# A gate's matmul folded into another projection as one more column, and a new hand-ordered list of steps, in a one-core kernel that mixes a state-space model with linear attention

## The chip, the core and the metric

The kernel runs on one core of a Trainium2 chip. The metric is the device time of one execution in microseconds (us); of several runs the median is taken. Each core has five engines with programs of their own: TensorE (PE in the profile; PEld is its loading of weights, which overlaps the matmuls), VectorE (DVE), ScalarE (ACT), GpSimd (POOL) and SyncE (SP, which here only starts DMAs). They meet through semaphores. Matmul results go to PSUM, eight banks of 128 x 512 f32; everything else lives in SBUF.

## The reference

x is 1 x 2048 x 512 in bf16 (2048 tokens). What is computed, cut to what matters:

```
g  = sigmoid(x @ gate_w)                              # one number per token
# a: diagonal complex state-space model, 512 states
Bu = x @ B_bar.T ;  h[t] = Lam_bar * h[t-1] + Bu[t]   # over the 2048 tokens
a  = 2 * Re(h @ C.T) + x * Dskip
# b: linear attention, 32 heads of 16, not causal
q, k, v = split(x @ wqkv)
phi(u)  = concat(softmax(u @ w_phi), softmax(-u @ w_phi))     # 32 features a head
kv = sum_t phi(k)[t] v[t].T ;  z = sum_t phi(k)[t]
o  = (phi(q) @ kv) / (phi(q) . z + eps)
b  = o @ wo
out = g * a + (1 - g) * b
```

## The kernel before, in words

**Tiles.** The tokens are cut into 16 tiles of 128; a tile holds one half of the tokens of one residue mod 8. On the side of q and of the output the tiles come in the order of the list `order`, so that n is a place and `ti = order[n]` the tile; k and v go through them as 0 to 15. Features are made for groups of tiles: k's in groups of 2, 2, 4, 4 and 4, q's in four groups of 4 (G0 to G3).

**Steps.** Every piece of work is a generator `st_*` or `feat_*`, and each `yield` ends a step. The string `ORDER` is the program: a token such as `k0` runs the next step of that generator, `@3` gives it PSUM bank 3 (`@51` the banks 5 and 1), and `:D` says that a copy or a scaling of this step goes to DVE and not to ACT. The last lines of the kernel walk through it:

```
for tok in ORDER.split():
    ...
    sel["eng"] = "dve" if eng == "D" else "act"
    sel["banks"] = [int(b) for b in banks]
    next(st[tok])
```

A manual schedule is on for all five engines: each of them executes its instructions in the order in which the list issues them, and waits where a buffer or a bank isn't ready. No planner moves anything. DMA queues work the same way: SP's loads, transposing loads and stores, and POOL's adding DMAs, go in list order.

**The names.** What the list's tokens do, in rough order of time:

- *Head.* `Lk` loads two of the four row blocks of k's weight on SP, while ACT's own queue has loaded the other two ahead of the list (`wk_nat`). `Z` is a matmul on zeros, used by no one (L316). `W00` and `W01` transpose the blocks that come by SP, `W10` and `W11` those that come by ACT's queue (L299), each with a copy out of PSUM; `T0`, `T1` transpose the first two tiles of x, the others come by transposing DMAs (`Lx`) into `xT`. `B` builds the block-diagonal matrix `BD` of w_phi. `f0` to `f3` multiply it into k's weight (L443), giving `Wk2`: 480 columns, 32 heads of 15, since a softmax needs only differences to the first feature. `w0` to `w3` do the same for q's weight, giving `Wq2`.
- *Projections.* `k`, `v`, `q` of a tile are each four matmuls of 128 x 128 weights (a block of `xT`) against 480 or 512 columns (`tile_mm`, L483), then a copy out of PSUM (`evac`, L129) into `Xq` or `vx`.
- *Features.* `x`, `n`, `e`, `s` for k and `X`, `N`, `E`, `S` for q: maximum and minimum over the features of a head as trees on DVE and the subtractions (L542, L548), exponentials on ACT (L554, two instructions of 2048 columns for four tiles), sums as a tree on DVE (L531), logarithm and exponential of the sums on ACT, and the multiplication on DVE (L569, L581). Four tiles of q then go through two transposing DMAs on SP into `phT`.
- *Keys and values.* `a` accumulates kv and z in two PSUM banks over all 16 tiles (L599). Between them stand the gate's matmuls (L603): four per tile with one column, into sixteen spare columns of the second bank. `Y` masks the sums into `KVm`.
- *Gate.* One generator `G` takes the sixteen columns from PSUM: a clamp on DVE, an exponential on ACT, an addition and a reciprocal on DVE (L743 on). It leaves `nge` (the clamped logit with its sign turned) and `G`, both 128 x 16, one column a tile.
- *State-space model.* `b` and `g` multiply x into the states and step through the eight residues on PE (L613, L625), `z` scans over the 256 chunks on DVE, `H`, `h`, `p` expand the result to all residues with scalings on ACT or DVE and, for j of 0 and 1, adding DMAs on POOL; `c` scales C, with an adding DMA (L648).
- *Output, per tile.* `y`: sixteen matmuls with C (L816) into a bank `py`; for tiles that aren't in `XD` four more against `Dd`, a diagonal matrix of Dskip (L823), so that x * Dskip is added in PSUM. `o`: eight matmuls of phi(q) with `KVm` (L835); on ACT the logarithm of the denominators (`ld`, L839) and an exponential with the bias `nge` (`rd`, L842), which makes exp(-logit) / denominator; on DVE the product `on` (L848). `O` transposes `on` by a DMA on SP into `oT` for two tiles (for one, at tiles 14 and 15). `t`: four matmuls with Wo (L875) accumulate on the same bank `py`; then `ot` = py * G on ACT (L881) or DVE (L883). That is the gate: G * (a + exp(-logit) * b) = g * a + (1 - g) * b. `R` stores two tiles.
- *Skip term of tiles in `XD`.* Before, `XD = (8, ..., 14)`: `u` makes `xd` = x * G * Dskip on DVE (L854), from token rows loaded by `Ld` into `WKV`, where the weights of k and v were; `t` then adds it with `scalar_tensor_tensor` on DVE (L879). Of tile 15, the last, PSUM and output are cut at column 384 (`LASTCUT`), so that the parts may go to two engines and two store queues.

Around the change, then, the order of the work is set by the list alone, and everything but the list is a few lines: those of the gate in `st_a` and `st_G`, and those that read `G` and `nge`.

Of the kernel before, what the change touches and what calls it, by code (L numbers as in the profile page):

```python
# [20 lines left out]
P = 128  # L21
# [8 lines left out]
b001@1 s0 x2 s0 s0 Lc b000 b101@3 x2 w3@4 k9 s0 n2 k13@2 x2 k10 b011 Lo n2 x2 n2 g001@7 M2 b010 b001 Lc e2 s1 x3 s1 n3  # L30
k14@5 x3 g000@1 v6 w1@0 s1 g001 x3 g000 n3 k13 s1 n3 g010@2 c1:D c1:D Lc Lc e2 g001 g010 s0 g000 s1 g011@6 g011 x0z:D
x3 n3 k14 c2 b101 D s1 s2 c2:D s2 g011 g010 g010 D g011 s2 a0@51 a0 c0 v2@7 w3 g011 g011 k12@3 c0:D w0@4 v2 g010 k12
g010 w2@6 w2 s2 g100@7 g100 x3 s2 n3 c3 c3:D x4 w1 Ld z0 z0 b110@6 x4 z0 n4 z0 w0 z0 n4 b111@2 g101@4 g101 s1 b110 z0
e3 g101 n4 q2@6 z0 n4 z0 q1@0 c3:D x4 z0 x4 e3 s3 z0 s3 g100 b111 c0 a1 a1 g111@4 s2 x4 n4 q3@3 g111 g111 g111 g110@2
H0:D g110 g110 q2 H0 c2 Ld Ld g110 s3 q0@6 b211@7 H0 s3 q1 s2 H0 g110 c0 q0 b201@0 q3 g110 c1 X0 N0 g111 g111 v7@6 H0
z1 z1 X0 s3 b200@2 g201@4 b201 N0 c2 v7 z1 X0 z1 z1 z1 s3 N0 b211 z1 b200 z1 g200@0 b210@6 g201 q4@7 e4 b210 X0 v4@2
N0 e4 z1 z1 H1 s2 g200 g200 g201 H1 g210@6 g211@3 g210 s4 H1 c1 g211 g210 q7@4 v4 s4 h0 h0 H1 H1 g210 h0 a2 a2 a2 a2
h1 h1 s4 s3 q4 s3 s4 g211 g211 q5@2 q5 q6@0 g211 X0 N0 q7 q6 g211 g210 X1 b300@7 g210 z2 b300 z2 p00:D z2 z2 z2 b311@4
p00 z2 b301@0 E0 X1 z2 b301 z2 E0 X1 v13@7 g301@6 s4 q9@0 b310@3 z2 b311 s4 z2 g301 g300@2 H2 S0 X1 S0 g301 g300 H2:D
S0 h1 b310 g310@4 g300 N1 S0 p10 c3 S0 h1:D h1 N1 s4 g311@6 q9 g311 g311 g311 g310 g310 g310 S0 S0 s4 p10 p10 H2 q10@2  # L40
g311 S0 g311 g310 g310 z3 z3 v13 H2 p00 H2 z3 z3 z3 v8@0 v8 v10@3 h0 z3 v10 p10 N1 v12@4 v12 z3 z3 S0 S0 h0 q8@0 p10
q8 z3 z3 v9@7 v9 v14@3 h2 h2:D H3:D H3:D p00:D v14 v15@0 v15 h2 v11@4 H3 a3 N1 a3 v11 a3 a3 a4 H3 q11@4 H3 a4 a4 h2 h2
a4 X1 N1 Y Y p11 h3 p11 y1@0 G y1 h3 y1 h3 Y Y q11 q10 X2 N2 G h3 h3 END q12@2 o1@4 o0@6 E1 X2 E1 o0 q14@1 q14 N2 o1
y6@3 y6 X2 N2 X2 S1 o0 o0 S1 q12 o1 y6 S0 p01 o1 q15@1 S1 N2 q15 q13@2 q13 p11 o3@6 y0@1 o3 S1 S1 p00 y0 X2 p30 o2@4
S1 o2 S1 o2 y0 N2 S1 o2 N3 o3 G Ld Ld E2 E2 y7@2 y7 S1 y7 y3@4 y3 y3 N3 p20 p01 X3 G o3 S2 O0 t0 t0 t1 t1 y5@5 S1 S1
X3 o4@6 O1 S2 o4 o4 N3 R0 o5@0 S2 S2 o5 o5 o4 o5 O2 S2 S2 N3 X3 X3 p30 y5 y5 y4@6 y4 S2 S2 o6@0 p01 p11 p01 o6 o6 X3
y2@7 p20 N3 E3 E3 p20 o6 p20 p20 t3 y2 y2 t2 t5 y4 t2 t3:D t4 t4 S2 S2 y10@4 o9@0 o9 o8@6 p30 p30:D p30 p11 y10 u9 S3
t5 o8 o8 o9 o8 o9 y11@5 o7@6 p01 y11 y9@0 S2 p21 S3 o7 S3 S3 O4 o7 o7 p31 p21:D y9 S3 S3 y8@1 S3 o10@6 R1 u8 o10 o10
S3 S3 y8 o10 p31 t8 o11@6 O3 t9 S3 S3 t6 o11 o11 p21 p31 t8 t9 y12@1 t7 p31:D y14@0 t6 t7 o11 o12@6 o12 p21 O5 p21
o13@2 u11 p31 y14 o12 o12 o13 y12 o13 R2 o14@6 o13 O6 o14 o14 o14 R4 u10 O7 y13@2 y13 o15@6 o15 o15 o15 t10 t10 R3 t11  # L50
t13 t11 u12 O8 u13 t12 t12 t13 u14 R5 t14 t14 R6 y15@54 y15 y15 t15 t15:D t15 R7 t15 R8 R8
# [4 lines left out]
XD = (8, 9, 10, 11, 12, 13, 14)  # L56
# [14 lines left out]
def kernel(  # L71
# [88 lines left out]
    Wq2 = const.tile([P, KT, DF], BF16, name="Wq2")  # L160
# [3 lines left out]
    gw_b = const.tile([P, KT], BF16, name="gw_b")  # L164
# [275 lines left out]
    def fold(W2, WT, dtile):  # L440
        pf = bank([P, DF], F32, "pf")
        for j in range(KT):
            MM(out=pf[:, j * DF // KT:(j + 1) * DF // KT], lhsT=WT[:, j, dtile * P:(dtile + 1) * P], rhs=BD[:, j].rearrange("p g f -> p (g f)"), start=True, stop=True)  # L443
# [37 lines left out]
    def tile_mm(pt, ti, W, k0=0, k1=KT):  # L481
        for kt in range(k0, k1):
            MM(out=pt[:], lhsT=xT[:, kt, ti * P:(ti + 1) * P], rhs=W[:, kt, :], start=(kt == 0), stop=(kt == KT - 1))  # L483
# [107 lines left out]
    def st_a(n):  # L591
        first, L = KGROUPS[n]
        for u in range(L):
            n_ = first + u
            ti = KO[n_]
# [6 lines left out]
            for kt in range(KT):  # L602
                MM(out=live["acc"][1][:, 4 * KVW + ti:4 * KVW + ti + 1], lhsT=xT[:, kt, ti * P:(ti + 1) * P],  # L603
                   rhs=gw_b[:, kt:kt + 1], start=False, stop=(n_ == NTI - 1 and kt == KT - 1), skip_group_check=True)
# [138 lines left out]
    def st_G():  # L743
        VS(out=nge[:], in0=live["acc"][1][:, 4 * KVW:4 * KVW + NTI], scalar1=-Z_MAX, scalar2=-1.0, op0=ALU.max, op1=ALU.mult)
        yield
        aexp(out=G[:], in_=nge[:], func=ACT.Exp)
        yield
        VS(out=G[:], in0=G[:], scalar1=1.0, scalar2=None, op0=ALU.add)
# [78 lines left out]
    def st_o(n):  # L827
        ti = order[n]
        op_ = pools["op"][1]
# [7 lines left out]
        yield  # L837
        ld = op_.tile([P, 2, 16], F32, name="ld")
# [3 lines left out]
        aexp(out=rd[:], in_=ld[:], func=ACT.Exp, scale=-1.0, bias=nge[:, ti:ti + 1])  # L842
# [8 lines left out]
    def st_u(n):  # L851
        ti = order[n]
        live["xd", n] = pools["op"][1].tile([P, D], F32, name="xd", bufs=2)
        nc.vector.scalar_tensor_tensor(out=live["xd", n][:], in0=xl(n), scalar=G[:, ti:ti + 1], in1=Drow[:], op0=ALU.mult, op1=ALU.mult)  # L854
# [11 lines left out]
    def st_t(n):  # L866
        ti = order[n]
# [5 lines left out]
        for py, (c, w) in zip(pys, [(0, D)] if len(pys) == 1 else LASTCUT):  # L873
# [4 lines left out]
            if n in XD:  # L878
                nc.vector.scalar_tensor_tensor(out=ot, in0=py[:], scalar=G[:, ti:ti + 1], in1=live["xd", n][:, c:c + w], op0=ALU.mult, op1=ALU.add)  # L879
            elif sel["eng"] == "act":  # L880
                nc.scalar.mul(out=ot, in_=py[:], mul=G[:, ti:ti + 1])  # L881
# [73 lines left out]
```

## Time and profile before

| | before |
|---|---|
| device time, median of 3 runs | 151.08 us (150.99 to 151.36) |
| span of the profiled execution | 149.4 us |
| PE busy | 142.8 us (96%), 1010 instructions |
| PE weight loads | 73.8 us (49%) |
| DVE busy | 139.0 us (93%), 338 instructions |
| ACT busy | 125.1 us (84%), 222 instructions |
| POOL busy | 26.6 us (18%), 42 instructions |
| DMA | 20.14 MB, mean 135 GB/s |

The profile records one execution, from its first instruction to its last (its span). The runs' median is 1.7 us longer than this span: a run's time also holds what lies around the span. A line of groups gives busy time, engine, source line, operation, output and inputs with their shapes, a count, and in brackets the idle time ahead of them with what ended it. A line of single rows begins with the start in us from the span's start and the duration. Matmuls overlap in the array, so a duration is longer than the distance to the next start; where costs are added up, distances are used.

### The profile page before, as it was taken

The numbers are of one execution on the slowest core, as the hardware profiler recorded it, in microseconds if no ns is written. First come the engines' busy times: TensorE is split into PE (matmuls) and PEld (weight loads), VectorE is DVE, ScalarE is ACT, GpSimd is POOL, SyncE is SP. The second block draws the span as 40 slices with busy tenths as digits, with TensorE's granted clock in tenths as the row PEclk, the third lists the DMA queues.
The fourth block names the chain that finished last, engine by engine and source line by source line (L and its number), as shares of the span: only waits on it lengthen the run. The fifth ranks groups of instructions, "written<-read, shape, count | busy, mean of one in ns | idle before, by whom it ended". The sixth has DMA issues, their size and how long they took to land.

```text
span 149.4 us, 2839 instructions
## 1 busy us (share of the span) xinstructions
PE 142.8 (96%) x1010; PEld 73.8 (49%) x1010; DVE 139.0 (93%) x338; ACT 125.1 (84%) x222; POOL 26.6 (18%) x42
## 2 busy tenths in 40 slices
PE   6999999999999999999999999999999999999980
PEld 2844444545545444464444467555444554455450
DVE  2899999999999999999999999999999999986880
ACT  3479999999999999999999999999989996552000
POOL 7403700000000341022605236011004200000000
PEclk9999999999999999999999999999999999999999
DMA  4999999991220174008274999908999996998742
GB/s 118 222 235 174 142 202 176 246 189 33 54 91 0 26 114 77 0 0 140 38 107 70 166 175 183 210 7 133 103 238 218 184 186 77 227 207 197 209 148 71
DMA packets 52959, 20.14 MB, mean 135 GB/s; under 512 B 44496, under 2 KB 52432, under 8 KB 52944
## 3 DMA queue, kind: packets, MB, share of 16 engines
q1 hardware_dynamic: 48000, 15.44, 53.1%
q0 software_dynamic: 4000, 4.20, 18.6%
q10 hardware_dynamic: 944, 0.31, 0.8%
q8 instruction: 8, 0.13, 0.4%
q14 instruction: 7, 0.06, 0.1%
HBM read 2.91 MB, written 2.10 MB: 33 GB/s over the span
## 4 chain that ended last, share of the span: by engine, by line
ACT 67%; PE 24%; issue 3%; DVE 2%
ACT EE L554 15%; PE PS L816 11%; ACT Xq L129 9%; PE PS L875 7%; ACT CT L436 6%; ACT vx L129 5%; ACT dg L436 4%; ACT H L129 3%; ACT vv L129 3%; ACT eb L129 3%; ACT Bn L129 3%; PE PS L316 2%; PE PS L835 2%; ACT lg L562 2%; ACT m L436 1%
## 5 line engine op out<-in xcount | busy, mean ns | idle before, releaser
L554 ACT ACTIVATE EE<-EE 128x2048 bf16<-128x2048 bf16 x16 | 32.5, 2066 | 0.2 <-DVE EE L548 0.2
L483 PE MATMUL PS<-WKV,xT 128*128 128x480 bf16 (+1 forms) x128 | 29.3, 373 | 0.2 <-DMA xT<-in_A_x_dram 0.2
L483 PEld LDWEIGHTS <-xT 128*128 128x128 bf16 x192 | 18.1, 98 | 19.4 <-DMA xT<-in_A_x_dram 0.7
L129 ACT CAST Xq<-PS 128x480 bf16<-128x480 f32 x32 | 20.1, 735 | 0.5 <-PE PS L483 0.5
L625 PE MATMUL PS<-xT,BT 128*128 128x512 bf16 x64 | 15.9, 379 | 0.0
L816 PE MATMUL PS<-C,H 128*128 128x512 bf16 x64 | 15.4, 378 | 0.5 <-DVE on L848 0.2
L875 PE MATMUL PS<-Wo,oT 128*128 128x512 bf16 (+2 forms) x68 | 15.5, 367 | 0.0
L613 PE MATMUL PS<-xT,BT 128*128 128x512 bf16 x64 | 15.4, 379 | 0.0
L483 PE MATMUL PS<-Wq,xT 128*128 128x480 bf16 x64 | 15.1, 366 | 0.0
L848 DVE TENSOR_TENSOR on<-PS,rd 128x512 bf16<-128x512 f32 x16 | 10.7, 681 | 2.3 <-ACT rd L842 2.3
L881 ACT ACTIVATE ot<-PS,G 128x512 bf16<-128x512 f32 (+1 forms) x8 | 4.9, 639 | 9.1 <-PE PS L875 9.1
L436 ACT ACTIVATE CT<-H,dgs 128x1024 bf16<-128x1024 bf16 x9 | 12.1, 1349 | 0.0
L129 ACT CAST vx<-PS 128x512 bf16<-128x512 f32 x16 | 11.7, 793 | 0.0
L648 POOL DMA_DIRECT2D C<-CT x4 | 5.4, 1352 | 35.0 <-ACT rc L566 31.8
L531 DVE TENSOR_TENSOR sm<-EE 128x2048 bf16<-128x2048 bf16 (+1 forms) x9 | 10.0, 1108 | 0.1
L542 DVE TENSOR_TENSOR EE<-Xq,mx 128x2048 bf16<-128x2048 bf16 (+1 forms) x9 | 10.0, 1109 | 0.0
L548 DVE TENSOR_TENSOR EE<-mn,Xq 128x2048 bf16<-128x2048 bf16 (+1 forms) x9 | 10.0, 1107 | 0.0
L613 PEld LDWEIGHTS <-BT 128*128 128x128 bf16 x64 | 6.3, 98 | 7.2 <-issue 0.2
L569 DVE TENSOR_TENSOR EE<-EE,rc 128x2048 bf16<-128x2048 bf16 x8 | 9.8, 1234 | 0.0
L625 PEld LDWEIGHTS <-BT 128*128 128x128 bf16 x64 | 6.1, 98 | 7.0
L875 PEld LDWEIGHTS <-oT 128*128 128x128 bf16 x68 | 6.1, 98 | 6.5 <-DMA oT<-on 0.5
L531 DVE TENSOR_TENSOR sm<-sm 128x512 bf16<-128x512 bf16 (+2 forms) x18 | 9.3, 516 | 0.0
(185 smaller groups left out, 325.8 us busy)
## 6 DMA issues: line engine op xcount, KB each, us to landing
out_dram<-ot SPq DMA_DIRECT2D x7, 256.0 KB, 2.4
C<-CT POOLq DMA_DIRECT2D x4, 256.0 KB, 3.9
eb<-CT POOLq DMA_DIRECT2D x4, 256.0 KB, 4.9
eb<-dg POOLq DMA_DIRECT2D x4, 256.0 KB, 5.9
WKV<-in_A_x_dram SPq DMA_DIRECT2D x3, 256.0 KB, 3.1
WKV<-in_B_wqkv_dram SPq DMA_DIRECT2D x1, 512.0 KB, 5.6
Wo<-in_B_wo_dram SPq DMA_DIRECT2D x1, 512.0 KB, 4.8
H<-CT POOLq DMA_DIRECT2D x2, 256.0 KB, 3.3
```

The costliest lines, as they stand in the source:

```text
L129: nc.scalar.copy(out=out_ap, in_=in_ap)
L436: nc.scalar.mul(out=out_ap, in_=in_ap, mul=s_)
L483: MM(out=pt[:], lhsT=xT[:, kt, ti * P:(ti + 1) * P], rhs=W[:, kt, :], start=(kt == 0), stop=(kt == KT - 1))
L531: VT(out=dst, in0=cur[:, :, :, 0:n, :], in1=cur[:, :, :, n:2 * n, :], op=op)
L542: VT(out=half(EE, 0), in0=X5, in1=live["mx", p].to_broadcast([P, L, 8, Dh, 4]), op=ALU.subtract)
L548: VT(out=half(live["EE", p], 1), in0=live["mn", p].to_broadcast([P, L, 8, Dh, 4]), in1=X5, op=ALU.subtract)
L554: aexp(out=EE[:, l_:l_ + 2], in_=EE[:, l_:l_ + 2], func=ACT.Exp)
L613: MM(out=pb[:], lhsT=BT[:, ri, kt, j * P:(j + 1) * P], rhs=cells(kt, 2 * pr), start=(kt == 0), stop=(kt == KT - 1))
L625: MM(out=pgq[:], lhsT=BT[:, ri, kt, js], rhs=cells(kt, r1), start=(kt == 0), stop=False)
L816: MM(out=py[:], lhsT=hs[j][ri], rhs=C2[:, 1 - ri, j, c:c + w], start=(j == 0 and ri == 0), stop=False)
L848: VT(out=live["on", g_][:, u], in0=pn[:, :, :, 0:Dh], in1=rd[:].unsqueeze(3).to_broadcast([P, 2, 16, Dh]), op=ALU.mult)
L875: MM(out=py[:], lhsT=oT[:, g, :], rhs=Wo[:, g, c:c + w], start=False, stop=(g == HG - 1))
```

## The change

*The gate.* `Wq2` becomes four columns wider (`DF + 4`, of which one is used: DF = 480). `gw` writes the gate's weight into its column 480 (the 481st). Q's projection of a tile then has 481 columns, and its last one is the gate's logit of that tile. `st_q` gets a third step, an `evac` of this one column into `nge`. The four matmuls a tile in `st_a` go. `G` becomes four generators `G0` to `G3`, each for four places of the q order, with the same four instructions on 128 x 4 instead of 128 x 16. Since q runs through places, `nge` and `G` are now indexed by the place n and not by the tile. `fold` and `tile_mm` get the slices that this needs.

*The skip term.* `XD` is (8, ..., 11): tiles 12 to 14 get their four `Dd` matmuls, and lose `u` on DVE and the addition in `t`. `Ld` has two loads of x fewer.

*The list.* `ORDER` was found anew, by a search with annealing over the steps; it differs nearly everywhere, in the order of the steps, the banks and the `:D` marks.

```diff
 ORDER = """
-Lk Lk Z@0 B:D B Z Z Z Z Z B B W01@1 Lx Z W00@2 Lx W00 W00 W01 W01:D Lx W11@3 W10@4 W11 Z B f1@5 f1 Lv f0@1 T1@0 W10:D
-f0:D T0@3 f2@2 T1 Lx T0:D f3@4 f3:D Lx f2 k1@6 Lx V@7 k0@3 V P k1 k1 U P U P2 Lx P2 U P2 P2 U P2 P4 P3 P4 k0 k0 n0 P4
...
-o13@2 u11 p31 y14 o12 o12 o13 y12 o13 R2 o14@6 o13 O6 o14 o14 o14 R4 u10 O7 y13@2 y13 o15@6 o15 o15 o15 t10 t10 R3 t11
-t13 t11 u12 O8 u13 t12 t12 t13 u14 R5 t14 t14 R6 y15@54 y15 y15 t15 t15:D t15 R7 t15 R8 R8
+Z@0 Z Z Z Lk Z Z W10@1 W11@2 W10 Lk Lx W00@3 B B Lx W11 B W00 B W00 W01@1 Lx W01 B T0@2 W01 f2@4 f1@3 V@1 Lx f2:D T0
+f0@5 Lx f3@6 f1 V P f3 T1@2 f0:D P P2 U Lv Z P2 T1 P2 Z P2 k0@3 k0 k1@6 P2 Lx P4 P4 k1 P4 i3 k5@2 i3 i0 P3 i0 P k2@0
...
+t8 p31 p31 y13@5 p31 y12 o12 o13@0 t9 O5 o13 y13 u10 y14 o13 o13 o14@0 y13 y14 G3 o14 o14 y12 t10 o14 R2 o15@0 t11
+u11 R3 o15 O6 o15 t10 y15@74 O7 y15 t13 R4 o15 t12 O8 G3 t11 t12:D y15 t14 t13 t14:D R5 R6 t15 t15 R7 t15 R8 t15 R8
 """
-XD = (8, 9, 10, 11, 12, 13, 14)
+XD = (8, 9, 10, 11)
...
-    Wq2 = const.tile([P, KT, DF], BF16, name="Wq2")
+    Wq2 = const.tile([P, KT, DF + 4], BF16, name="Wq2")
...
-    gw_b = const.tile([P, KT], BF16, name="gw_b")
...
     def st_gw():
-        nc.vector.tensor_copy(out=gw_b[:], in_=vec[:, 4, :])
+        nc.vector.tensor_copy(out=Wq2[:, :, DF], in_=vec[:, 4, :])
...
-            MM(out=pt[:], lhsT=xT[:, kt, ti * P:(ti + 1) * P], rhs=W[:, kt, :], start=(kt == 0), stop=(kt == KT - 1))
+            MM(out=pt[:], lhsT=xT[:, kt, ti * P:(ti + 1) * P], rhs=W[:, kt, 0:pt.shape[-1]], start=(kt == 0), stop=(kt == KT - 1))
...
     def st_q(n):
-        pq = bank([P, DF], F32, "pq")
+        pq = bank([P, DF + 1], F32, "pq")
         tile_mm(pq, order[n], Wq2)
         yield
-        evac(xrel(n), pq[:].rearrange("p (hh x) -> p hh x", hh=8))
+        evac(xrel(n), pq[:, 0:DF].rearrange("p (hh x) -> p hh x", hh=8))
+        yield
+        evac(nge[:, n:n + 1], pq[:, DF:DF + 1])
         yield
...
-            for kt in range(KT):
-                MM(out=live["acc"][1][:, 4 * KVW + ti:4 * KVW + ti + 1], lhsT=xT[:, kt, ti * P:(ti + 1) * P],
-                   rhs=gw_b[:, kt:kt + 1], start=False, stop=(n_ == NTI - 1 and kt == KT - 1), skip_group_check=True)
...
-    def st_G():
-        VS(out=nge[:], in0=live["acc"][1][:, 4 * KVW:4 * KVW + NTI], scalar1=-Z_MAX, scalar2=-1.0, op0=ALU.max, op1=ALU.mult)
+    def st_G(g):
+        ns = slice(4 * g, 4 * g + 4)
+        VS(out=nge[:, ns], in0=nge[:, ns], scalar1=-Z_MAX, scalar2=-1.0, op0=ALU.max, op1=ALU.mult)
         yield
...
-        aexp(out=rd[:], in_=ld[:], func=ACT.Exp, scale=-1.0, bias=nge[:, ti:ti + 1])
+        aexp(out=rd[:], in_=ld[:], func=ACT.Exp, scale=-1.0, bias=nge[:, n:n + 1])
```

In the new list the steps `u8` to `u11` remain, `gw` stands later, and `G0` to `G3` stand among the products of the end, where before one `G` stood behind `Y`.

More of the change, by code (lines that the diff above doesn't have):

```diff
@@ L30 @@
[L30 to L44, printed above, removed]
@@ L837, in st_o @@
         yield
+        op_ = pools["op"][1]
         ld = op_.tile([P, 2, 16], F32, name="ld")
@@ L851, in st_u @@
     def st_u(n):
-        ti = order[n]
         live["xd", n] = pools["op"][1].tile([P, D], F32, name="xd", bufs=2)
-        nc.vector.scalar_tensor_tensor(out=live["xd", n][:], in0=xl(n), scalar=G[:, ti:ti + 1], in1=Drow[:], op0=ALU.mult, op1=ALU.mult)
+        nc.vector.scalar_tensor_tensor(out=live["xd", n][:], in0=xl(n), scalar=G[:, n:n + 1], in1=Drow[:], op0=ALU.mult, op1=ALU.mult)
         yield
@@ L866, in st_t @@
     def st_t(n):
-        ti = order[n]
         pys, oT = live["py", n], live["oT", n]
```

53 lines of the change are left out of this document (33 added, 20 removed).

## The prediction

> **What bounds the kernel now.** I read the page's first part, then its slices and its chain, then the stages, and last the order of time on each engine at the places where the new list differs.
>
> ```profile
> PE 142.8 (96%) x1010; PEld 73.8 (49%) x1010; DVE 139.0 (93%) x338; ACT 125.1 (84%) x222; POOL 26.6 (18%) x42
> ACT  3479999999999999999999999999989996552000
> ACT 67%; PE 24%; issue 3%; DVE 2%
> 40.00:70.00 30.00, 29.91 (x209) 15.07 (x207) 30.00 (x63) 30.00 (x51) 5.45 (x5) 1.00 0.30 57
> 120.00:149.40 29.40, 24.95 (x190) 12.94 (x188) 22.94 (x40) 11.20 (x29) 0.00 (x0) 1.00 0.79 165
> ```
>
> The page's first part shows three full engines, the slices (40 of 3.7 us) that ACT's share falls off after slice 32. The chain's row gives ACT 67%, but that means only that ACT never paused, not that it alone limits: the stage from 40 to 70 us (columns: time, then PE, PEld, DVE, ACT, POOL) has PE, DVE and ACT all busy for 30 us of 30. From 120 us on ACT has let go (11.2 of 29.4) and PE sets the end. So an edit is worth something only if all three engines can follow it: work off PE alone helps if DVE and ACT deliver as early as PE asks.
>
> **The gate column, on PE.** PE overlaps its matmuls, so a price is the step from one start to the next.
>
> ```profile
> 91.56 0.24 PE L603 MATMUL PS<-gw_b,xT 128*128 128x1 bf16 x4
> 91.66 0.41 PE L599 MATMUL PS<-vx,EE 128*128 128x68 bf16 x8
> 98.17 0.39 PE L823 MATMUL PS<-Dd,xT 128*128 128x128 bf16 x4
> 98.39 1.78 PE L483 MATMUL PS<-Wq,xT 128*128 128x480 bf16 x8
> 100.01 0.42 PE L835 MATMUL PS<-KVm,phT 128*128 128x68 bf16 x8
> 138.03 4.32 PE PS L875 x20
> 142.35 1.75 PE PS L816 x16
> 144.10 0.22 PE PS L823 x4
> ```
>
> Four gate matmuls take 91.66 - 91.56 = 0.10 us, so the 16 groups that go give -1.6. A projection matmul of 480 columns takes (100.01 - 98.39)/8 = 0.2025, one of 512 takes 4.32/20 = 0.216: a column is 0.42 ns, and 64 matmuls with one column more give +0.03. Nothing shows an odd width; the wider form bounds it, 64 x 0.0135 = +0.9, and nothing makes it a gain. I take +0.03, the nearer width.
>
> **The skip term, on PE and DVE.** Tiles 12 to 14 get their four Dd matmuls back: 98.39 - 98.17 = 0.22 each, +0.66. PE's work in sum: -1.6 + 0.03 + 0.66 = **-0.9**.
>
> ```profile
> 139.26 1.40 DVE L879 SCALAR_TENSOR_TENSOR ot<-PS,G,xd 128x512 bf16<-128x512 f32 x2
> 140.58 1.40 DVE L854 SCALAR_TENSOR_TENSOR xd<-WKV,G,Drow 128x512 f32<-128x512 bf16 x2
> 105.52 0.17 DVE L748 TENSOR_SCALAR G<-G 128x16 f32<-128x16 f32 x1
> 105.60 0.69 DVE L581 TENSOR_TENSOR EE<-EE,rho 128x1024 bf16<-128x1024 bf16 x1
> ```
>
> DVE loses three xd and three ot with an addend, at 0.66 each (two ot start at 139.26, two xd at 140.58): -4.0. It gains one plain ot (tile 14, while tile 15's first part goes to ACT), and the sigmoid's three small steps stand there four times instead of once: nine more at 0.08 (105.52 to 105.60) make +0.7, at twice that where one needs the one before it +1.4, and not below nothing. I take 1.0. Copies and scalings change sides both ways and about cancel. But most of what goes lies behind the last feature group, where DVE has room (22.9 of 29.4). What counts is the work ahead of G3's last multiply: there the list puts the xd of tiles 8 and 9 behind it (-1.3), one plain ot goes to ACT (-0.7), the small steps add some 0.5: **-1.5**.
>
> **Queues.** Two loads of x into WKV go from SP; the one ahead of Wo waits for the last k product, which the new list has long before Wo's first use in t0. R4 stands ahead of O8, with its tiles done before o15. On POOL one fill of Xq moves ahead of Dd, and the adding DMAs are reordered among p and h sums. I cost these at 0: what hides them is that their readers stand several us behind; without that cover each would cost its wait in full.
>
> **The gate column, on ACT.** Sixteen evacuations of one column and three more small exponentials are new.
>
> ```profile
> 97.13 0.42 ACT L839 ACTIVATE ld<-PS 128x32 f32<-128x32 f32 x1
> 97.21 0.80 ACT L129 CAST Xq<-PS 128x480 bf16<-128x480 f32 x1
> 110.21 0.20 ACT L839 ACTIVATE ld<-PS 128x32 f32<-128x32 f32 x1 [0.47 <-PE PS L835]
> 110.44 0.32 ACT L842 ACTIVATE rd<-ld,nge 128x32 f32<-128x32 f32 x1
> 103.84 3.71 ACT L554 ACTIVATE EE<-EE 128x2048 bf16<-128x2048 bf16 x2 [0.15 <-DVE EE L548]
> 107.84 1.22 DVE L531 TENSOR_TENSOR sm<-EE 128x2048 bf16<-128x2048 bf16 x1
> 115.96 3.70 ACT L554 ACTIVATE EE<-EE 128x2048 bf16<-128x2048 bf16 x2
> 120.98 1.22 DVE L531 TENSOR_TENSOR sm<-EE 128x2048 bf16<-128x2048 bf16 x1
> ```
>
> A small read of PSUM on ACT costs 0.08 where nothing after it needs it (97.13 to 97.21) and 0.23 where the next does (110.21 to 110.44). So 16 cost 1.3 to 3.7, and not less than nothing, for they replace nothing on ACT. I take 0.08: in the new list mostly other work follows them. PE's next user of that bank now waits for this second read as well. Ahead of G2's exponentials ACT also has two copies of W and one of xT more (some 0.5 each, the rows of the head below), an o tile's two steps and a sigmoid's one: 1.3 + 1.5 + 0.6 = +3.4. It gains about 1.4 at the head. So these exponentials end 2.0 later, at 109.4 (before at 103.84 + 3.6). DVE takes up their sums, at 107.84 before, later too: by the head's 0.7 and by G3's first subtraction of about 1.1, which now stands ahead, so at 109.6. No cover is left; I take **+0.3** between 0 and the 1.0 of a few copies at the dearer price. At G3 there is more: before, the exponentials ended near 119.6 and the sums began at 120.98.
>
> **The list, at the head.** The new list starts with the two W blocks that come over ACT's own DMA.
>
> ```profile
> 1.26 2.74 PE L316 MATMUL PS<-warm 128*128 128x512 bf16 x6 [1.26 <-DVE warm L148]
> 3.79 0.42 PE L299 MATMUL PS<-ident,C 128*128 128x128 bf16 x2
> 4.43 1.70 PE L299 MATMUL PS<-ident,C 128*128 128x128 bf16 x14
> 5.92 0.63 PE L316 MATMUL PS<-warm 128*128 128x512 bf16 x1
> 6.35 0.63 PE L443 MATMUL PS<-BD,Xq 128*128 128x120 bf16 x8
> 7.91 0.58 PE L483 MATMUL PS<-WKV,xT 128*128 128x480 bf16 x2
> 19.42 1.85 PE L483 MATMUL PS<-WKV,xT 128*128 128x480 bf16 x8 [0.17 <-DMA xT<-in_A_x_dram]
> 1.29 0.53 ACTq L151 DMA_DIRECT2D C<-in_B_wqkv_dram  x1
> C<-in_B_wqkv_dram ACTq DMA_DIRECT2D x1, 256.0 KB, 3.5
> 5.10 1.23 ACT L129 COPY Xq<-PS 128x512 bf16<-128x512 bf16 x2 [1.96 <-PE PS L299]
> ```
>
> That DMA is issued at 1.29 and lands 3.5 later, at 4.8; before, the first transposes began at 3.79 with the rows that SP loads. Sixteen transposes at 0.107 ((5.92 - 4.43)/14) end at 6.5 instead of 5.92. All four W copies now stand on ACT, one behind the other, at some 0.5 to 0.6 (the 5.10 row): the last is done near 7.5, the folds after it by 8.2, the copy of one of them on DVE by 8.8. So the first k matmul starts at 8.8, not 7.91. Between k0's two halves before lost 0.2 waiting for the copies of the folds; I take **+0.7** for PE and DVE. ACT, which now loses less time between its first copies, is the 1.4 ahead. Five transposes of x come before Lv and the last two behind two of B: the wait for xT that showed as 0.17 (a gap of 0.3 between starts) goes, **-0.3**.
>
> **In the middle** I find no place where the new list leaves an engine long idle, but DVE, not PE, is what is late next: its work up to the multiply of G3 is 1.5 shorter, but it starts 0.7 later and has the 0.3 of G2. PE needs its products (the copies out of the o banks, the p sums) and comes 0.9 sooner in work itself, so it can't run ahead of DVE: I take PE's waits there as before's, with G2's 0.3 on top.
>
> **The list, at the end.**
>
> ```profile
> 137.62 0.42 PE L835 MATMUL PS<-KVm,phT 128*128 128x68 bf16 x8
> 140.09 1.20 SPq L862 DMA_TRANSPOSE oT<-on  x1
> 144.24 0.88 PEld L875 LDWEIGHTS <-oT 128*128 128x128 bf16 x8
> 145.11 0.62 DVE L883 TENSOR_SCALAR ot<-PS,G 128x384 bf16<-128x384 f32 x1 [0.30 <-PE PS L875]
> 145.33 0.37 ACT L881 ACTIVATE ot<-PS,G 128x128 bf16<-128x128 f32 x1 [6.71 <-PE PS L875]
> ```
>
> From o15's matmuls (137.62) its result goes over ACT and DVE to the transposing DMA (140.09), and t15 takes it at 144.24. PE covers that with 4.32 + 1.75 + 0.22 = 6.29 of other matmuls and arrives just as the weights do. In the new list t10 stands ahead of o15, which leaves 5.42: 0.87 less. If the way takes what it took, PE waits up to 0.9; if the DMA lands in 3.4 after its issue, nothing. I take +0.2. t15's two parts go through ACT one behind the other instead of through DVE and ACT side by side: +0.2, between 0 and the 0.62 of the first part.
>
> **Sum:** -0.9 + 0.7 - 0.3 + 0.3 + 0.2 + 0.2 = +0.2 on a span of 149.4, so 149.6. The runs' median, 151.08, stands 1.7 above that span; I keep that: **151.3**, which is no change within 0.3% (0.45 us, about what a measurement of this kernel tells from none).
>
> **Rivals.** *PE's work alone decides (faster).* PE is the fullest engine; if the later head is made up (DVE's lighter load speaks for it) the -0.9 and the -0.3 remain: 149.9; with four more short waits gone, each like the 0.17 for xT, 149.2. Against it: DVE's rows at 93% and no engine with room to catch up.
>
> *The one-column copies sit in ACT's way (slower).* At 0.23 each ACT reaches G2's exponentials 2.4 later than summed; the 0.4 of cover there ends, DVE takes up its sums about 2 later and everything behind follows: 153.1. It decides from 0.1 each on. For it: ACT's 84% is nearly all before 120 us.
>
> *The array warms late (slower).* The rows show PE at half rate at first: a warm matmul of 512 columns at 5.92 still lasts 0.63, where later ones step at 0.216, and the folds at 6.35 are the first at full rate, after 5.1 us without a pause. The new list pauses from 3.8 to 4.8. If full rate then comes 3 us later, the k matmuls from 8.8 on cost 0.4 instead of 0.2: about 1 us, of which DVE passes on most: 152.3. [...]
>
> **How the numbers follow.** About even, 150.6 to 152.0 on its own: 0.45. PE's work decides: 0.25. One-column copies: 0.13. Late warming, or other waits that the new order brings on PE for ACT: 0.17. Faster by over 0.3%: the second case and 0.10 of the first, 0.35. Same: 0.20, all of the first. Slower: 0.15 of the first and both last, 0.45. The range reaches from the second case with its short waits gone to the dear copies, 149.2 to 153.1.
>
> **What would show it.** No L603 group; Q's matmuls still stepping at 0.2025; one-column copies on ACT at 0.08 to the next start. The first k near 8.8 and full rate by then. No idle for xT at 19. G2's sums on DVE waiting for ACT by under 1 us; more means the copies are dear. A wait of t15's weights for oT of 0 to 0.9 at the end. Wrong altogether would be a PE whose groups of idle time, short in before, are many and put down to ACT's copies: then the new order itself costs more than any term above.

## The result: 4.5% slower

The changed kernel takes 158.15 us (median of 4 runs, 157.45 to 158.48), the kernel before on the same chip 151.07: a ratio of 1.0449, with a 95% interval of 1.0416 to 1.0482. The forecast was 151.3, in a range of 149.2 to 153.1. The profiled execution took 157.45, its span 155.8, which is 6.4 more than before. In what follows ratios are of undisturbed runs alone and medians of all runs, so that a median can lie above what its ratio gives.

**The page of the changed kernel**, its first part, its slices and its chain:

```profile
PE 142.5 (92%) x942; PEld 72.8 (47%) x958; DVE 140.4 (90%) x340; ACT 128.5 (83%) x245; POOL 29.0 (19%) x42
PE   6899797999999999999999999798959979999990
ACT  3688979999999999999999998799996989722212
DVE 63%; PE 20%; DMA 9%; issue 5%; ACT 1%; ACTq 0%; DVEq 0%
```

PE is as busy as before (142.5 against 142.8) although it has 52 matmuls less (the gate's 64 gone, 12 with `Dd` more) and, by the forecast's sum, 0.9 us of work less. The row counts 942 matmuls because 16 are missing from this trace; the weight loads, one for each matmul, are all there, 958 against 1010. What has turned round is the chain: 67% ACT before, 63% DVE now. The stages of the changed kernel, and then the same stages of before (time, then PE, PEld, DVE, ACT, POOL with their instructions):

```profile
10.00:30.00 20.00, 17.72 (x81) 7.88 (x82) 19.11 (x64) 17.46 (x33) 3.00 (x6) 1.00 1.12 179
30.00:90.00 60.00, 58.90 (x374) 29.35 (x379) 59.41 (x123) 59.37 (x109) 11.73 (x13) 1.00 0.37 69
90.00:120.00 30.00, 26.76 (x205) 13.94 (x207) 28.94 (x68) 27.12 (x56) 8.23 (x7) 1.00 0.94 142
```

```profile
10.00:30.00 20.00, 19.84 (x99) 9.15 (x98) 19.88 (x70) 19.95 (x40) 3.86 (x11) 1.00 1.07 189
30.00:90.00 60.00, 59.80 (x415) 30.39 (x414) 59.92 (x137) 60.00 (x104) 12.09 (x11) 1.00 0.46 80
90.00:120.00 30.00, 29.54 (x259) 16.10 (x256) 29.90 (x62) 29.28 (x46) 6.07 (x5) 1.00 0.93 160
```

From 10 to 30 us PE and ACT stand still for 2.3 and 2.5 of 20, from 90 to 120 for 3.2 and 2.9 of 30. DVE shows few pauses, and in the middle stage gets through fewer instructions, 123 instead of 137 (their sizes differ, so this is a hint only). If DVE holds the others up, as the chain says, it does so while it counts as busy.

**Where DVE's time goes.** VectorE's row of the changed kernel, G1's sums (start, duration), and then the same sums in the kernel before:

```profile
94.96 1.21 DVE L533 TENSOR_TENSOR sm<-EE 128x2048 bf16<-128x2048 bf16 x1
96.21 1.15 DVE L533 TENSOR_TENSOR sm<-sm 128x1024 bf16<-128x1024 bf16 x2
97.28 0.42 DVE L682 TENSOR_TENSOR ms<-w,T2s 128x512 bf16<-128x512 bf16 x1
```

```profile
97.50 1.23 DVE L531 TENSOR_TENSOR sm<-EE 128x2048 bf16<-128x2048 bf16 x1
98.64 0.68 DVE L848 TENSOR_TENSOR on<-PS,rd 128x512 bf16<-128x512 f32 x1
99.24 0.68 DVE L531 TENSOR_TENSOR sm<-sm 128x1024 bf16<-128x1024 bf16 x1
```

Before, the first sum ends at 97.50 + 1.23 = 98.73, and the next instruction, which does not read it, has started at 98.64: 0.09 ahead of that end. In the new list the second step of the tree stands directly behind the first and reads its result: it starts at 96.21, 0.04 after the end at 96.17. Over all instructions of DVE the starts fall into these two heaps, 0.08 or a little more ahead of the end of the one before, or some 0.035 after it, with little between. I call the second kind *held*: against the other it costs 0.12 us, of which 0.08 lies inside rows that count as busy.

That gives an account of DVE up to the end of G3's last multiplication. Held starts (0.01 to 0.075 after the end before) are counted with what they cost against a start 0.08 ahead, idle are the later ones, and work is the rest, from the span's start. Ten of the held starts of each kernel are fills and constants in its first 5 us, which read nothing of the one before; they cancel in the differences. Of the changed kernel's other 59, 58 read the tile that the instruction before them wrote.

| kernel | last multiplication of G3 ends | work | held starts | idle | from there to the span's end |
|---|---|---|---|---|---|
| before | 127.97 | 122.57 | 26: 3.14 | 2.26 | 21.5 |
| changed | 134.39 | 121.41 | 69: 8.02 | 4.96 | 21.4 |
| difference | +6.42 | -1.16 | +4.88 | +2.70 | -0.1 |

The whole loss lies ahead of G3's last multiplication, and behind it next to nothing is lost or won. DVE has 1.16 less work, 43 more held starts, and 2.7 more idle, of which 1.0 is in the head, where it waits 1.31 for the first fold of k's weight instead of 0.30. Between 18 and 110 us the kernel before has not one held start, the changed one has 33.

### The profile page after: what moved, and what is told of

Read it like the earlier page. It is cut to its first block, busy times and chain, and to the rows that moved or that the text cites. A ratio compares the mean times of both kernels' runs of the same rounds, so it can differ in the third digit from the quotient of the medians.

```text
span 155.8 us, 2753 instructions
## 1 busy us (share of the span) xinstructions
PE 142.5 (92%) x942; PEld 72.8 (47%) x958; DVE 140.4 (90%) x340; ACT 128.5 (83%) x245; POOL 29.0 (19%) x42
## 4 chain that ended last, share of the span: by engine, by line
DVE 63%; PE 20%; DMA 9%; issue 5%; ACT 1%; ACTq 0%; DVEq 0%
PE PS L815 8%; DVE sm L533 8%; PE PS L871 8%; DMA oT<-on 7%; DVE mn L533 7%; DVE mx L533 6%; DVE EE L571 5%; DVE EE L544 5%; DVE EE L550 3%; DVE w L676 3%; DMA C<-in_B_wqkv_dram 2%; DVE dg L429 2%; DVE EE L583 2%; DVE on L846 2%; PE PS L832 1%
## 5 line engine op out<-in xcount | busy, mean ns | idle before, releaser
L556 ACT ACTIVATE EE<-EE 128x2048 bf16<-128x2048 bf16 x16 | 30.5, 1928 | 1.7 <-DVE EE L550 1.7
L130 ACT CAST Xq<-PS 128x480 bf16<-128x480 f32 x31 | 16.9, 577 | 0.0
L611 PE MATMUL PS<-xT,BT 128*128 128x512 bf16 x64 | 16.0, 379 | 0.8 <-ACT Xq L130 0.7
L623 PE MATMUL PS<-xT,BT 128*128 128x512 bf16 x64 | 16.2, 378 | 0.3 <-ACT eb L130 0.3
L483 PE MATMUL PS<-Wq,xT 128*128 128x481 bf16 x64 | 15.3, 366 | 1.1 <-DVE KVm L758 1.0
L646 POOL DMA_DIRECT2D eb<-dg x4 | 6.2, 1552 | 31.9 <-ACT dg L436 15.2
L877 ACT ACTIVATE ot<-PS,G 128x512 bf16<-128x512 f32 (+2 forms) x11 | 6.6, 639 | 6.7 <-PE PS L871 6.7
L837 ACT ACTIVATE ld<-PS 128x32 f32<-128x32 f32 x16 | 3.2, 197 | 8.1 <-PE PS L832 7.9
L130 ACT CAST vx<-PS 128x512 bf16<-128x512 f32 x16 | 9.5, 614 | 0.2 <-PE PS L483 0.2
```

The lines of the kernel that those rows point to most:

```text
L130: nc.scalar.copy(out=out_ap, in_=in_ap)
L556: aexp(out=EE[:, l_:l_ + 2], in_=EE[:, l_:l_ + 2], func=ACT.Exp)
L611: MM(out=pb[:], lhsT=BT[:, ri, kt, j * P:(j + 1) * P], rhs=cells(kt, 2 * pr), start=(kt == 0), stop=(kt == KT - 1))
L623: MM(out=pgq[:], lhsT=BT[:, ri, kt, js], rhs=cells(kt, r1), start=(kt == 0), stop=False)
```

## The experiments

All are timed against the kernel before on the same chip. "List" is `ORDER`; steps are moved in it so that only VectorE's own order changes, unless something else is said.

**1. Steps moved apart in the new list.** The tokens of VectorE's steps change places with those near them.

```diff
-i0 Lx Lb x0 i3 n0 n0 n0 k2 i0 i1 i1 x0 x0 x0 x0z P3 i2 i2 k7
+i0 Lx Lb i3 n0 x0 k2 i0 i1 n0 x0 i1 n0 x0 x0z P3 i2 x0 i2 k7
...
```

> The changed kernel with its list, but VectorE's steps moved by up to two places among each other, so that a step seldom stands directly behind the one whose result it reads: 21 such neighbours in the list instead of 64. All else is as in the changed kernel. Theory A (neighbours: such a step starts some 0.03 us after the end of the one before it, all others some 0.08 us before that end, so each costs 0.12, and VectorE sets the pace): 43 x 0.12 = 5 us less, about 153. Theory B (the sixteen one-column copies sit in ScalarE's way): no change, 158. Theory C (the new order of the engines against each other, waits across engines): no change, 158, or 1 us less at most.

Measured: 156.99 (156.72 to 157.19), ratio 1.0379 (1.0356 to 1.0403): 1.2 less, not 5. Held starts fall from 69 to 31, and idle rises from 4.96 to 9.28. The moves had been made without regard to what a step waits for: steps that wait for ACT could be drawn forward, and products be put behind sums that were not due. That this made the idle is not shown; some 0.7 of it is the first load, which landed later in this profiled execution (last section).

**2. Steps put close in the old list.** The same the other way round, in the kernel before.

```diff
-k0 k0 n0 P4 x0 P P2 P3 i1 k2@7 k3@6 k2 k3 x0 i1 i1 x0 n0 i0
+k0 k0 n0 x0 P4 P P2 P3 i1 k2@7 k3@6 k2 k3 x0 x0 i1 i1 n0 i0
...
```

> The kernel before with its list, but VectorE's steps moved by up to two places among each other, so that a step often stands directly behind the one whose result it reads: 64 such neighbours instead of 22. All else is as before. Theory A (neighbours): 42 x 0.12 = 5 us more, about 156. Theory B (one-column copies): no change, 151, since it has none. Theory C (order across engines): 151 to 152.

Measured: 157.11 (157.04 to 157.78), ratio 1.0398 (1.0371 to 1.0426): 6 more.

**3. The control to it.** As many steps are moved (77), as far, with the neighbours kept at 22.

```diff
-k3 x0 i1 i1 x0 n0 i0 i1 i0 V2@3 V2 i1 M x0 k5@4 i0 k7@5 k7 i0 n0 k4@2
+k3 x0 i1 i1 i0 x0 i1 n0 i0 V2@3 V2 i1 n0 M x0 k5@4 i0 k7@5 k7 i0 k4@2
...
```

> The control to the old list with close neighbours: the kernel before, with as many of VectorE's steps moved (77 of 317, by up to two places under the same rules), but with the number of neighbours kept at 22. If it is the neighbours that cost 6 us there: 151 to 152. If any disturbance of VectorE's order costs as much: 155 to 157.

Measured: 153.05 (153.02 to 153.14), ratio 1.0132 (1.0117 to 1.0148): 2 more. If the moves of experiment 2 disturbed the order as much as these, two of its 6 us are the disturbance of an order that was tuned, and four are the neighbours. The account of DVE, as above, bears this out: both have about 1.9 more idle than before (2.26), and they differ in the held starts.

| kernel | last multiplication of G3 ends | work | held starts | idle |
|---|---|---|---|---|
| old list, steps close | 134.81 | 122.92 | 67: 7.82 | 4.07 |
| old list, shuffled | 130.20 | 122.70 | 27: 3.27 | 4.23 |

The two differ by 40 held starts and 4.6 us, at 0.12 each or a little less, and most of it arrives at the end (157.11 - 153.05 = 4.1; the profiled execution of the close one took 157.78, with the clock at half for 3.4 us, last section). The chains of the two, the close one first, don't tell them apart:

```profile
DVE 41%; PE 28%; ACT 17%; DMA 6%; issue 4%; ACTq 0%; DVEq 0%
DVE 47%; PE 22%; ACT 20%; issue 4%; DMA 4%; DVEq 0%
```

DVE has the largest share in both, and more of it in the control: the chain says that DVE is late, and not why.

**4. The gate column in the old list.** The code of the changed kernel, `XD` as before, the old list with a third step of `q` and the sigmoids added.

```diff
-q2 H0
+q2 q2 H0
...
-y1@0 G y1
+y1@0 G0 G1 y1
...
```

> The gate as column 481 of Q's weight and the sigmoid for four tiles at a time, in the list of before: each one-column copy stands on ScalarE right behind the copy of its tile, the four gate matmuls of a tile are gone; the skip term stays on VectorE for tiles 8 to 14. Theory A (neighbours): the list's neighbours are those of before, so 151, or down to 150 if TensorE's 1.6 us count. Theory B (one-column copies): most of the 7 us, 154 to 158. Theory C (order across engines): 151.

Measured: ratio 1.0146 (1.0087 to 1.0206); single runs from 152.69 to 158.69. The column costs something in the old list, about 2 us, but not the 7.

**5. The same with the skip term of four tiles.**

> As the gate column in the list of before, and the skip term on VectorE for tiles 8 to 11 alone: tiles 12 to 14 get their four diagonal matmuls back, VectorE loses three products and three additions, the list keeps its order otherwise. Theories A and C: 150.5 to 151.5 (the matmuls cost 0.66 at the end, where TensorE sets it). Theory B: 154 to 158. If the skip term were the cause: 1 us or more above the gate column alone.

Measured: ratio 1.0261 (1.0168 to 1.0353), runs from 154.02 to 156.89. The scatter leaves open how much the skip term adds here.

**6. The skip term alone in the old list.**

```diff
-XD = (8, 9, 10, 11, 12, 13, 14)
+XD = (8, 9, 10, 11)
...
-t13 t11 u12 O8 u13 t12 t12 t13 u14 R5 t14 t14
+t13 t11 O8 t12 t12:D t13 R5 t14 t14:D
```

> The kernel before, with the skip term on VectorE for tiles 8 to 11 alone: three times four diagonal matmuls more on TensorE, three products and three additions less on VectorE, two loads of x less; the list else as before. If TensorE sets the end from 120 us on: 0.66 more, 151.6. If VectorE's relief there counts: 150.5. Neither is near the 7 us.

Measured: 151.81 (151.63 to 152.64), ratio 1.0057 (1.0036 to 1.0077): 0.8 more, near the 0.66 of twelve matmuls where PE sets the end.

**7. The new list with the old gate.** The kernel before with the new list: `q` has two steps again, `gw` stands ahead of `a0`, one `G` behind `Y`.

```diff
-b111 q3 q2 q2 z0 q0@7
+b111 q3 q2 z0 q0@7
...
-g010 s0 g000 a0@64 n3
+g010 s0 g000 gw a0@64 n3
...
```

> The new list with the gate as before: one-column matmuls beside the kv sums, one sigmoid for all tiles, no one-column copies; the skip term stays as in the changed kernel. If the list makes the loss: 157 to 158.5 (the copies took 0.05 each in the profile of the changed kernel, 0.8 in sum, and the matmuls' 1.6 come back on TensorE, which waits there anyway). If the gate column makes it: 151 to 153.

Measured: 159.06 (157.65 to 159.77), ratio 1.0522 (1.047 to 1.0574). Three of its four runs had a granted clock of 0.989 (last section); the fourth, at 0.999, took 157.65, within the changed kernel's runs. Without the column the new list is no faster. So the list makes the loss, not the column; the skip term, which is in this kernel too, costs 0.8 alone in the old list (experiment 6).

**8. Steps moved apart gently in the new list.** Only up to 115 us, past no product and no copy, and nothing drawn forward that waits for another engine: 31 neighbours.

```diff
-i0 i0 Lx Lb x0 i3 n0 n0 n0 k2 i0 i1 i1 x0 x0 x0 x0z P3 i2 i2 k7
+i0 n0 i0 Lx Lb i3 n0 x0 n0 k2 i0 x0 i1 x0 i1 x0 x0z P3 i2 n0 i2 k7
...
```

> The changed kernel with VectorE's steps moved apart again, but gently: only up to G3's subtractions (115 us), never past a product or a copy, and no step that waits for another engine is drawn forward. 31 neighbours in the list instead of 64. If VectorE's neighbours alone are the loss: 33 x 0.12 = 4 us less, 154. If ScalarE is as late as VectorE in the new list (it waited for nothing from 46 to 96 us): 156 to 157.5. If the first attempt lost its gain by the moves behind 115 us alone (it was 1.3 ahead at 126 us and level at 134): 155.5 to 156.5.

Measured: 155.32 (154.98 to 155.41), ratio 1.0282 (1.026 to 1.0304): 2.8 less for 31 fewer held starts, 0.09 each. In the profiled execution the first load came late (last section), which adds some 1.1 to its idle.

**9. The head of before on the new list.**

```diff
-Z@0 Z Z Z Lk Z Z W10@1 W11@2 W10 Lk Lx W00@3 B B Lx W11 B W00 B W00 W01@1 Lx W01 B
+Lk Lk Z@0 B:D B Z Z Z Z Z B B W01@1 Lx Z W00@2 Lx W00 W00 W01 W01:D Lx W11@3 W10@4
...
```

> The changed kernel with the first steps in the order of before, up to the folds of k's weight: the blocks that come by SP are transposed first, three copies out of PSUM and more go to VectorE again; behind that the new list goes on. If the head's delay (0.7 forecast; TensorE stood 0.7 later at 8 us in the profile) goes through to the end: 157.2 to 157.5. If it is covered later: 158. If the late start draws more behind it (TensorE lost 2.7 more from 15 to 30 us): 155 to 156.5.

Measured: 158.16 (158.04 to 158.3), ratio 1.0475 (1.0454 to 1.0495): nothing. DVE has 0.7 less idle than in the changed kernel (4.26 against 4.96), but 1.0 more work (122.42 against 121.41), since three copies go from ACT to it.

**10. Both, apart and the head of before.**

> Both: the steps moved gently apart and the head of before. If the two are separate causes that add up: the gains of the two single runs in sum, some 152.5 to 154.5. If something else in the new list sets the pace behind them (ScalarE's own order, transfers): 155.5 or more.

Measured: 154.28 (154.2 to 154.6), ratio 1.0221 (1.0199 to 1.0242): 3.9 less than the changed kernel. The cleanest pair of all is this kernel and that of experiment 9, on the same chip: the same instructions, in the same order on every other engine than DVE. It has 32 held starts fewer and takes 3.9 us less (158.16 against 154.28), 0.12 each. The head, worth nothing alone, gives 1.0 against experiment 8. G1's sums in this kernel:

```profile
92.23 1.21 DVE L533 TENSOR_TENSOR sm<-EE 128x2048 bf16<-128x2048 bf16 x1
93.37 0.28 DVE L684 TENSOR_TENSOR H<-mc,ms 128x256 bf16<-128x256 bf16 x1
93.57 0.68 DVE L533 TENSOR_TENSOR sm<-sm 128x1024 bf16<-128x1024 bf16 x1
94.17 0.28 DVE L686 TENSOR_TENSOR H<-mc,ms 128x256 bf16<-128x256 bf16 x1
```

Each step starts ahead of the end of the one before it: 93.37 against 92.23 + 1.21 = 93.44.

| kernel | last multiplication of G3 ends | work | held starts | idle |
|---|---|---|---|---|
| new list, old head (experiment 9) | 134.69 | 122.42 | 69: 8.01 | 4.26 |
| new list, apart gently | 132.00 | 121.30 | 38: 4.51 | 6.19 |
| new list, apart, old head | 130.88 | 122.42 | 37: 4.36 | 4.10 |

Between the first and the last row the work is the same and the idle nearly so; the held starts make 3.65 of the 3.81.

**11. What the two other parts do in this repaired list.** The old gate in it:

> The new list with VectorE's steps moved apart and the head of before (154.3), and the gate as before: one-column matmuls, one sigmoid, no one-column copies. If the column costs 1.4 there, as it does in the old list (the two kernels with the scalings moved differ by that): 153. If TensorE's 1.6 more count in a list in which it waits less: 154.5 to 156.

Measured: 155.63 (155.1 to 157.26), ratio 1.0316 (1.0253 to 1.0379), 1.3 above the repaired list. Two of its runs, 156.08 and 157.26, had a granted clock of 0.989 and 0.987; the other two took 155.10 and 155.18, 0.9 above. So the gate column is a gain there, of a size that these runs leave open. The skip term of seven tiles in it (`u12` to `u14` back, two loads of x more, twelve matmuls less):

> The repaired new list (154.3) with the skip term on VectorE for tiles 8 to 14 as before, twelve diagonal matmuls less, and the last sigmoid finished before its products. If these matmuls stand on the path that ends last, 12 x 0.056: 153.6. If VectorE's three products and additions hold up the last tiles instead: 154.3 to 155.5; the earlier form of this kernel, which multiplied with an unfinished gate, took 156.7.

Measured: 155.85 (155.25 to 158.1), ratio 1.0298 (1.0271 to 1.0325), by the ratios 1.2 above. So the skip term of four tiles is a gain there as well. An earlier form, in which `u12` multiplied by a gate that was not yet finished, so that its output is not the reference's, had nearly the same expectation and took 156.74 (155.89 to 158.5):

> The same repaired list (154.3) with the skip term on VectorE for tiles 8 to 14 as before, twelve diagonal matmuls less. If these matmuls stand on the path that ends last, 12 x 0.056: 153.6. If VectorE's three products and additions hold up the last tiles instead: 154.3 to 155.5.

**12. ACT's scalings moved, with the gate column and without.** The steps `p01 p11 p01`, three scalings ahead of G3's exponentials that feed POOL's last adding DMAs, go behind them.

```diff
-o6@0 p01 p11 p01 o6 o6 X3 y2@7 p20 N3 E3 E3 p20
+o6@0 o6 o6 X3 y2@7 p20 N3 E3 E3 p01 p11 p01 p20
```

> The gate column in the list of before once more, and ScalarE's three scalings that feed POOL's last adding DMAs moved behind G3's exponentials, so that those DMAs no longer run beside the transposing DMA of G2 (10.8 us for its two parts there, TensorE waited 4.6 for it). If that meeting made the spread (152.7 to 158.7) and most of the loss: 151 to 152.5, all runs within 0.5. If the gate column costs it by itself: 153 to 155 as before.

Measured: 154.68 (154.32 to 155.43), ratio 1.0246 (1.0211 to 1.0281). Without the column:

> The kernel before with the same three scalings moved behind G3's exponentials, and nothing else. ScalarE has 1.8 us of them in front of these exponentials. If ScalarE sets the pace there (G3's subtraction done well ahead): 1 us less, 150. If VectorE's subtraction is as late: 151. If the later adding DMAs hold up the products with C of tiles 12 to 15: 152 or more.

Measured: 153.29 (152.65 to 154.54), ratio 1.0157 (1.0106 to 1.0208). The move itself costs 2.3. In the kernel with the column it brings a new wait:

```profile
122.58 1.24 ACT L877 ACTIVATE ot<-PS,G 128x512 bf16<-128x512 f32 x2
123.88 0.41 PE L832 MATMUL PS<-KVm,phT 128*128 128x68 bf16 x8 [2.11 <-ACT ot L877]
```

The moved scalings now stand ahead of ACT's output copies, and PE waits 2.1 for the bank that these free; in the kernel without the column it waits as long there. Whether the transposing and the adding DMAs had hindered each other this does not show; that stays open. The difference of the two kernels, 1.4, prices the column in the old list.

**13. The old list's own last neighbours moved apart.** Five of them, between 100 and 126 us.

```diff
-o5@0 S2 S2 o5 o5 o4 o5 O2 S2 S2 N3 X3 X3 p30
+o5@0 S2 o5 o5 o4 o5 S2 O2 S2 S2 X3 N3 X3 p30
...
```

> The kernel before with five of its own last neighbours on VectorE (between 100 and 126 us) moved apart, by at most two places each. By their price 5 x 0.12 = 0.6 less on VectorE; if it is on the path: 150.4 to 150.8. If ScalarE and TensorE set the pace there: 151. If the moved steps hold up a product: 151.5 or more.

Measured: 152.99 (152.85 to 153.23), ratio 1.0125 (1.0105 to 1.0145): 1.9 more, though four held starts fewer. DVE and ACT of this kernel, and then of the kernel before:

```profile
111.26 1.29 DVE L848 TENSOR_TENSOR on<-PS,rd 128x512 bf16<-128x512 f32 x2 [0.38 <-ACT rd L842]
112.47 0.41 DVE L531 TENSOR_TENSOR smf<-sm 128x256 f32<-128x256 bf16 x1
112.91 0.42 ACT L562 ACTIVATE lg<-smf 128x256 f32<-128x256 f32 x1 [1.25 <-DVE smf L531]
```

```profile
110.57 0.42 DVE L531 TENSOR_TENSOR smf<-sm 128x256 f32<-128x256 bf16 x1
110.91 1.28 DVE L848 TENSOR_TENSOR on<-PS,rd 128x512 bf16<-128x512 f32 x2
111.10 0.40 ACT L562 ACTIVATE lg<-smf 128x256 f32<-128x256 f32 x1
```

Before, the last sum of G2 stands directly behind the step it reads, is held, and ends at 110.99. Moved behind two products it ends at 112.88, ACT waits 1.25 for it, and everything behind is 1.8 later. So a held start can be worth paying where another engine waits for the result.

No kernel here beats the kernel before.

## Why the prediction was wrong, and where it was right

- **What bounds the kernel.** That all three engines are full up to 120 us and that DVE is late next held. So did the remark that PE's lighter work can't run ahead of DVE.
- **The step that failed** is DVE's account: "its work up to the multiply of G3 is 1.5 shorter". The work is 1.16 shorter, near the forecast. But I took work for time: I added durations by kind, with distances to the next start from rows of before, where from 18 to 110 us no start is held, and put what the new order itself costs DVE at nothing. The new list has 43 more held starts: +4.9 of the 6.4 in the account. Moving 31 apart gave 2.8 back, 32 with the head of before 3.9, and making 40 in the old list cost 4.1. The order of DVE's instructions in the new list showed them before any run. I saw the dearer price only for the sigmoid's three small steps ("at twice that where one needs the one before it"), and did not ask it of the trees.
- **The sentence on the middle**, "I take PE's waits there as before's", fell with it: PE lost 2.1 more from 10 to 30 us and 2.8 more from 90 to 120. The term for G2, +0.3, was not there: in the changed kernel G2's exponentials end at 115.37, DVE takes up their sums at 116.03 and does not wait for them; both come 6 us later than forecast.
- **The gate column on PE.** No group of the old gate is left. The wider matmuls of q:

```profile
L483 PE MATMUL PS<-Wq,xT x64: 363/367/368, 47.1 to 102.7; 128*128 128x481 bf16 x64
```

From start to start they take 0.204 on average (0.203 in the median), q's of before 0.202: +0.1 for 64: the nearer width was right. The 1.6 saved did not show as time: in the new list PE waits for others instead, and in the old one the column costs on balance.
- **The gate column on ACT.** A copy of one column, and the next start:

```profile
60.92 0.19 ACT L130 COPY nge<-PS 128x1 f32<-128x1 f32 x1
60.97 0.41 ACT L130 CAST vv<-PS 128x256 bf16<-128x256 f32 x1
```

0.05, below the 0.08 forecast, and so for 15 of the 16; the rival of the dear copies is out. Yet in the old list, where ACT is the chain, the column costs 1.4, nearly twice what these copies add up to (0.8); why, no run settles.
- **The skip term.** 0.8 in the old list, 0.66 forecast; a gain of 1.2 in the repaired new one. That DVE's products and additions weigh more there, since it is late, is argued and not shown.
- **The head.** The first k was forecast near 8.8. The changed kernel's first rows:

```profile
4.55 1.89 PE L299 MATMUL PS<-ident,C 128*128 128x128 bf16 x16 [0.56 <-DMA C<-in_B_wqkv_dram]
6.70 0.89 PE L443 MATMUL PS<-BD,Xq 128*128 128x120 bf16 x8
7.34 0.66 DVE L132 CAST WKV<-PS 128x480 bf16<-128x480 f32 x1 [1.31 <-PE PS L443]
7.63 0.59 PE L443 MATMUL PS<-BD,Xq 128*128 128x120 bf16 x8
8.76 0.78 PE L483 MATMUL PS<-WKV,xT 128*128 128x480 bf16 x3
```

It starts at 8.76. The head of before alone gave nothing (experiment 9), since what DVE saved in idle it got in copies; with DVE's steps apart it gave 1.0 (experiment 10). How much of this is the order and how much the first load, which came at 5.6 instead of 4.55 in the profiled execution without it, is not shown.
- **The wait for xT** is gone, as forecast, and gained nothing that shows: at 20.6 PE waits 0.29 for a copy on ACT.
- **The end.** From G3's last multiplication to the end 21.4 against 21.5: the two terms of 0.2, with the skip term's matmuls, did not show.
- **The late warming** came, and cost little. The folds at 6.70 still last 0.89 for 8, those at 7.63 take 0.59 and step at full rate, later than before (6.35); but that is over when the first k comes. The 3 us later were a guess of mine; by these rows it is at most 1.3. That PE's pause did it this pair can't show: in the fourteen profiled executions with the head of before the full rate comes anywhere from 4.0 to 7.3 us, in the four with the new head from 7.2 to 9.0, 2.7 to 3.7 behind PE's restart. The transposes show the scatter of one and the same head: in the median they last 0.219 in experiment 9 and 0.314 in the kernel before.
- **The rivals.** The slower side had 0.45, but none of its mechanisms had this size. What the prediction named last, that "the new order itself costs more than any term above", is what happened, with DVE's neighbours in the place of ACT's copies.

**What stays open.** The repaired list with the old head is still 3.3 us above the kernel before. In DVE's account it has 11 held starts more (+1.2) and 1.8 more idle, and PE waits 1.5 and 0.8 us in it for a transposing DMA of `oT`, at 111 and 121 us, where the kernel before has no pause of PE above 0.4 after its first 2 us. The gate column and the skip term are gains there, so it is the order; which moves of it, no run tells. The control (2 us for 77 moves that keep the neighbours) and experiment 13 (1.9 us for a few) show how much a list near its best loses by any disturbance, so that a rest of this size need not have one cause.

## What to carry to other kernels

Where the order of an engine's instructions is written by hand or found by a search, price a VectorE instruction that reads the result of the one directly ahead of it at 0.12 us more than any other, which is what these traces show (a start 0.035 after that one's end instead of 0.08 ahead of it); count such neighbours in both orders before costing anything else. Put an independent step between them, except where another engine waits for the result. An engine that is 90% busy in the profile may be losing 5% of the span (here 8.0 of 155.8 us), mostly in rows that look busy: count its held starts. The chain's share does not show them (63% for DVE in the changed kernel, but 47% in the control and 64% in the repaired list).

## What the runs showed of the hardware

- VectorE's starts fall into two heaps: some 0.08 us ahead of the end of the instruction before (245 of 339 in the changed kernel, 293 of 337 before, between 0.07 and 0.145), or 0.035 after it where its result is read. 40 of the second kind made 4.1 us in the kernel's time (experiments 2 and 3), and 32 of them 3.9 where nothing else differs (9 and 10).
- The load of half of k's weight over ACT's queue, issued near 1.3 us in every execution, lands 3.2 to 4.4 us later in the eighteen profiled executions. The list that starts with it shows that; its transposes in another execution, of the kernel with the steps gently apart:

```profile
L299 PE MATMUL PS<-ident,C x16: 287/314/315, 5.6 to 7.2; 128*128 128x128 bf16 x16
```

They begin at 5.6 instead of 4.55. In the four profiled executions with the new head the first one starts at 4.55, 5.3, 5.3 and 5.6; in all fourteen with the head of before, which starts with SP's loads, at 3.8.
- Behind some pauses of PE its clock was low for a while. In six of the eighteen profiled executions the granted clock falls to half in the middle of the kernel, for 3.4 us, in the kernel of experiment 4 for 6.8; the mean clock of these six is 0.972 to 0.989, that of the other twelve 0.994 to 1.0. PE's pause in experiment 4, and the clock's row there:

```profile
126.17 1.09 PE L832 MATMUL PS<-KVm,phT 128*128 128x68 bf16 x16 [4.60 <-DMA phT<-EE]
PEclk9999999999999999999999999999999857999997
```

Each time PE has stood still for 1.95 to 4.6 us, and the half clock begins in that pause or at most 0.8 us behind it; a pause of 2.11 (experiment 12, with the column) and all of 1.64 or less left the clock full. That the pause makes it is likely by this and not shown: no run changes the pause alone. With the old gate in experiment 11 eight matmuls with Wo take 3.57 behind a pause of 2.44, at the half clock; eight in experiment 4 take 1.89 at the full one. A window of 3.4 us at half in a span of 156 is a mean clock of 0.989, which three runs of experiment 7 have; in experiments 4, 5 and 7, and with the old gate in 11, the runs with a mean clock of 0.989 or less are the longest ones; in experiment 8 one of 0.989 is not.
